# Attention and channel mix on one core: units of two pairs in one cycle, the receptance unit ahead of the last keys' scores, two gather steps on VectorE

## The chip, the cores and the metric

The kernel runs on one core of one Trainium2 chip. The metric is the device time of one execution in microseconds (us); three executions give a median. The profile is of one further execution. TensorE (PE in the profile) multiplies, with its weight loads shown apart as PEld; VectorE is DVE, ScalarE is ACT, SyncE (SP) issues all loads and stores, GpSimd (POOL) does almost nothing here.

## The reference

```python
# q, k, v: (8, 12, 448, 64); x: (8, 448, 768) after the heads are joined
scores = q @ k.transpose(0, 1, 3, 2) / sqrt(64) - log(448)
x = sigmoid(scores) @ v                       # heads joined to 768 columns
x_prev = x shifted by one row, first row zero
xk = mu_k * x + (1 - mu_k) * x_prev
xr = mu_r * x + (1 - mu_r) * x_prev
k  = maximum(xk @ w_k, 0)                     # 768 -> 1024
v  = k * k @ w_v                              # 1024 -> 768
r  = 1 / (1 + exp(-(xr @ w_r)))               # 768 -> 768, "receptance"
out = r * v
```

The scores carry a sigmoid and no sum over a row, so each block of keys can be weighed alone.

## The kernel before

Two heads make a pair: 48 pairs, six to each of the eight batch entries. Keys are cut into three chunks of 128 and a tail of 64. For one pair, `scores` (L322) multiplies a chunk of keys with all 448 queries of both heads, three times, because each operand is split into a high half and a low half (`kh`, `kl`, `qh`, `ql`; `prepare`, L295 the cast on ScalarE, L296 the rest on VectorE). The two heads use the two halves of the array's rows (64x128 in the profile). The result lies in a tile `sc` of two PSUM banks, one per head; there are three such tiles, used in turn. `sigmoid` (L343, ScalarE) turns it into `pf`. `score_tail` (L331) does the 64 last keys of both heads in one 128x128 multiplication into bank 0 of the next `sc`, and its sigmoid makes `pt`. `weigh` (L351) multiplies `pf` with the values into `av`, in 128x64 halves; `weigh_tails` (L360) adds the tails of two pairs in 64x64 quarters. So four shapes of the array are in use, and the order decides how often the shape changes.

`gather` takes a finished pair out of `av`: a copy `xx` (L369) and its store to `x_d`, a multiplication by 1 - mu_r into `t` (L371), the addition of the shifted part (L372, VectorE), and the split into `xr` high (L374, ScalarE) and low (L375, VectorE). The copy and the multiplication are on ScalarE.

`receptance` is one unit of xr @ w_r: six blocks of three matmuls (L386 to L388), 18 in all, into bank 1 of the `sc` tile whose bank 0 has the tail's scores; then a sigmoid `ro` (L392) and a store to `r_d`. 48 units are needed; 40 are done one per pair from pair 7 on, the other eight behind attention.

Meanwhile the weights, stored as 64-bit numbers, are turned into 32-bit ones by VectorE (`convert`, L222 to L226, from the raw words `wraw`), w_r first (L243, L244 split it into `slot`), then w_k and w_v, which `convert_seven` combines to the seven products of a fast matrix multiplication and stores to HBM. `load_weight` fetches such a product back (`wop`), and L411 and L412 split it into a slot.

Behind attention a second plan prepares the first right-hand sides (`ys`, `rr`) and runs the last eight units. A third plan is the channel mix itself (L592), both stages.

The order is not written by hand. Each step is entered in a plan with an engine, a cost in ns and a due time (`at`, counted in pairs); `Plan.order` runs a list schedule over the engines, lowest due time first, and emits the instructions in that order. TensorE's steps are chained, so their order is that in which the program enters them. Waits follow from the tiles, and a tile counts as a whole: a matmul that writes bank 1 of an `sc` tile waits for an earlier emitted sigmoid that reads bank 0 of it. Each engine takes its instructions strictly in order.

Of the kernel before, what the change touches and what calls it, by code (L numbers as in the profile page):

```python
# [8 lines left out]
F32 = mybir.dt.float32  # L9
# [88 lines left out]
def attention_then_channel_mix(  # L98
# [15 lines left out]
    P = 128  # L114
# [36 lines left out]

    WP, PFB, PTB, LEAD = 512, 6, 4, 2
    WR_PACE, W_PACE = 0.45, 0.75
    LATE = 2
# [157 lines left out]

    def turn(n, c):
        return (n * (NC + 1) + c) % 3

    def scores(n, c, at):
        u = turn(n, c)

        def go():
            for e, (kk, qq) in enumerate(products(n)):  # L320
                for h in range(2):
                    nc.tensor.matmul(sc[u][:, h, :S], kk[half[h], c * P:(c + 1) * P], qq[half[h], :], start=e == 0, stop=e == 2)  # L322

        pe(mm(3) + SWITCH * (c == 0), go, qk(n), [("sc", u, 0), ("sc", u, 1)], at)

    def score_tail(n, at):
        u = turn(n, NC)

        def go():
            for e, (kk, qq) in enumerate(products(n)):  # L330
                nc.tensor.matmul(sc[u][:, 0, :S], kk[:, NC * P:], qq, start=e == 0, stop=e == 2)  # L331

        pe(mm(3) + SWITCH, go, qk(n), [("sc", u, 0)], at)

    def sigmoid(n, c, at):
        u = turn(n, c)
        if c < NC:
# [8 lines left out]
    def weigh(n, c, at):  # L346
# [5 lines left out]

        pe(900 + SWITCH * (c == 0), go, [("pf", i), ("vn", n % 5)], [("av", n % 2)], at)


    def weigh_tails(n, at):
# [5 lines left out]
        reads = [x for m in (n, n + 1) for x in (("pt", m % PTB), ("vn", m % 5))]  # L362
        pe(950, go, reads, [("av", 0), ("av", 1)], at)

    def gather(n, at):
        b, j = divmod(n, NP)
        x, y = xx[n % 2], t1[n % 2]
        X, T = ("xx", n % 2), ("t1", n % 2)
        op(ACT, act(S), at, lambda: nc.scalar.copy(x[:, 1:], av[n % 2][:, :S]), [("av", n % 2)], [X])  # L369
        dma(x_d[j][b], x[:, 1:], at, [X], [("x_d", n)])  # L370
        op(ACT, act(S, True, True), at, lambda: nc.scalar.mul(y, x[:, :S], omr[:, j:j + 1]), [X, ("om", 0)], [T])  # L371
        op(DVE, dve(S, ptr=True), at, lambda: nc.vector.scalar_tensor_tensor(y, x[:, 1:], mur[:, j:j + 1], y, ALU.mult, ALU.add), [X, T], [T])  # L372
# [4 lines left out]
    def receptance(b, i, at, bank):  # L377
# [3 lines left out]
        for j in range(NJ):  # L381
# [8 lines left out]
            nh = i * P // HN  # L390
            pe(mm(3), go, keys + [("wr", j, nh), (("wr", j, nh), "lo")], [tk], at)
        op(ACT, act(S), at, lambda: nc.scalar.activation(ro[u], t[:, :S], AF.Sigmoid), [tk], [("ro", u)])  # L392
        dma(r_d[i][b], ro[u], at, [("ro", u)], [("r_d", i, b)])

# [21 lines left out]
    prepare(0, -9)  # L416
    load(1, -8)
    for i, (t, src, om) in enumerate(((mur, mu_r, omr), (muk, mu_k, omk))):
        dma(t, src, -2, [], [("mu", i)])
        op(DVE, 75, 0, lambda t=t, om=om: nc.vector.tensor_scalar(om, t, -1.0, 1.0, ALU.mult, ALU.add), [("mu", i)], [("om", i)])  # L420
    jt = 0.0
    for nh in range(2):
        for j in range(NJ):
            convert_wr(j, nh, jt)
            jt += WR_PACE
    jt = max(6, jt)
    for w, out7, half_rows, n in ((w_k, wk_o, NJH, DF // 2), (w_v, wv_o, NFH, HN)):
# [280 lines left out]
```

## Time and profile before

| | us |
|---|---|
| three executions | 930.02, 929.22, 929.09 |
| median | 929.22 |
| profiled execution, its own time | 932.01 |
| span of that execution | 930.2 |
| mean granted clock of TensorE | 0.99 |

The page's slices show the stages (each digit is the busy share of 1/40 of the span in tenths):

```profile
PE   6889999999999999999989999999999999999998
DVE  5999877852222232222225789696968978695955
ACT  5785666655565666556555756556464533233330
DMA  7679997863333434334127556334365556465514
```

Attention fills the first 21 slices, about 480 us. VectorE and the DMA engines are heavily used only in the first eight or nine of them, where the weights are converted. From slice 22 on the channel mix keeps TensorE full. A wait is given with the instruction that ended it; a group of instructions with its mean duration in ns and the idle time of the engine ahead of it. The time of a matmul is from its start to a modelled end, and matmuls overlap: the distance from one start to the next tells what one costs.

### The profile page before, as it was taken

What the parts mean: (1) busy time and instruction counts of PE and PEld (TensorE: products, weight loads), DVE (VectorE), ACT (ScalarE), POOL (GpSimd) and SP (SyncE); (2) the same over time, 40 slices, a digit from 0 to 9 for tenths busy, and PEclk for the clock granted to TensorE, in tenths of its full rate; (3) what the DMA queues carried; (4) which work ended last, traced back from release to release, by engine and by line L of the source; (5) the groups of instructions that cost most, each with busy time, mean ns of one, the idle gap of its engine ahead of it and who ended that gap; (6) DMA issues with size and microseconds to landing.
All of it is one profiled execution on the core that took longest, in us unless ns stands there. A gap on an engine that the chain in (4) does not pass through costs nothing.

```text
span 930.2 us, 13102 instructions
## 1 busy us (share of the span) xinstructions
PE 879.8 (95%) x4656; PEld 684.6 (74%) x4656; DVE 572.9 (62%) x1039; ACT 500.4 (54%) x858; POOL 0.5 (0%) x8
## 2 busy tenths in 40 slices
PE   6889999999999999999989999999999999999998
PEld 3446566656665666566558899999999999999997
DVE  5999877852222232222225789696968978695955
ACT  5785666655565666556555756556464533233330
POOL 0000000000000000000000000000000000000000
PEclk8899999999999999999999999999999999999999
DMA  7679997863333434334127556334365556465514
GB/s 257 205 252 335 302 318 241 280 215 102 122 115 103 135 111 132 102 106 130 50 92 245 175 174 197 119 139 129 125 228 161 199 163 216 132 196 178 159 60 148
DMA packets 90929, 159.21 MB, mean 171 GB/s; under 512 B 10352, under 2 KB 73328, under 8 KB 90864
## 3 DMA queue, kind: packets, MB, share of 16 engines
q1 hardware_dynamic: 90864, 158.38, 52.6%
q8 instruction: 36, 0.59, 0.3%
q14 instruction: 29, 0.24, 0.1%
HBM read 99.62 MB, written 58.72 MB: 170 GB/s over the span
## 4 chain that ended last, share of the span: by engine, by line
PE 91%; ACT 4%; DVE 2%; issue 2%; DMA 1%; SPq 0%; POOLq 0%; POOL 0%; ACTq 0%; DVEq 0%
PE xb L592 25%; PE yb L592 19%; PE av L351 12%; PE sc L322 10%; PE sc L386 7%; PE sc L388 6%; PE sc L387 6%; PE sc L331 4%; ACT pt L343 2%; PE av L360 2%; DMA wraw<-in_moe_w_r 1%; DVE wbits L226 0%; SPq L210 0%; ACT t L371 0%; ACT pf L343 0%
## 5 line engine op out<-in xcount | busy, mean ns | idle before, releaser
L386 PE MATMUL sc<-xr,slot 128*128 128x448 f32 x288 | 110.7, 384 | 30.9 <-ACT pt L343 25.3
L517 ACT CAST rr<-ys 128x448 fp32r<-128x448 f32 x135 | 73.9, 567 | 105.0 <-PE yb L592 40.6
L343 ACT ACTIVATE pf<-sc 128x896 f32<-128x896 f32 x144 | 122.7, 920 | 12.7 <-PE sc L322 12.7
L351 PE MATMUL av<-pf,vn 128*64 128x448 f32 x576 | 121.4, 557 | 0.0
L372 DVE SCALAR_TENSOR_TENSOR t<-xx,mur,t 128x448 f32<-128x448 f32 x48 | 30.7, 681 | 136.7 <-ACT t L371 136.7
L387 PE MATMUL sc<-xr,slot 128*128 128x448 f32 x288 | 105.9, 368 | 0.0
L388 PE MATMUL sc<-xr,slot 128*128 128x448 f32 x288 | 105.8, 367 | 0.0
L592 PE MATMUL xb<-rr,slotb 128*128 128x448 f32 x450 | 93.4, 365 | 0.7 <-issue 0.7
L592 PE MATMUL yb<-rr,slot 128*128 128x448 f32 x450 | 93.9, 364 | 0.0
L296 DVE TENSOR_TENSOR kl<-kn,kh 128x512 fp32r<-128x512 f32 x48 | 33.1, 690 | 97.2 <-ACT kh L295 97.2
L386 PEld LDWEIGHTS sc<-xr,slot 128*128 128x128 f32 x288 | 54.4, 189 | 51.8 <-ACT pt L343 40.2
L518 DVE TENSOR_TENSOR rr<-ys,rr 128x448 fp32r<-128x448 f32 x135 | 80.4, 618 | 19.5 <-ACT rr L517 19.4
L592 PEld LDWEIGHTS xb<-rr,slotb 128*128 128x128 f32 x450 | 84.4, 188 | 7.7 <-issue 1.1
L592 PEld LDWEIGHTS yb<-rr,slot 128*128 128x128 f32 x450 | 84.4, 187 | 6.7
L351 PEld LDWEIGHTS av<-pf,vn 128*64 128x64 f32 x576 | 37.8, 139 | 61.5 <-issue 60.4
L322 PE MATMUL sc<-qh,kh 64*128 64x448 f32 x288 | 59.6, 410 | 7.5 <-ACT qh L295 6.6
L392 ACT ACTIVATE ro<-sc 128x448 f32<-128x448 f32 x48 | 26.2, 545 | 67.4 <-PE sc L388 59.9
L322 PE MATMUL sc<-ql,kh 64*128 64x448 f32 x288 | 55.1, 379 | 6.0 <-DVE ql L296 6.0
L343 ACT ACTIVATE pt<-sc 128x448 f32<-128x448 f32 x48 | 26.1, 545 | 60.7 <-PE sc L388 55.7
L388 PEld LDWEIGHTS sc<-xr,slot 128*128 128x128 f32 x288 | 54.5, 189 | 4.6
L387 PEld LDWEIGHTS sc<-xr,slot 128*128 128x128 f32 x288 | 54.6, 190 | 3.6
L322 PE MATMUL sc<-qh,kl 64*128 64x448 f32 x288 | 54.1, 372 | 1.1 <-DVE kl L296 1.1
(88 smaller groups left out, 1410.0 us busy)
## 6 DMA issues: line engine op xcount, KB each, us to landing
k_d<-cc SPq DMA_DIRECT2D x64, 224.0 KB, 2.0
kn<-in_k SPq DMA_DIRECT2D x48, 256.0 KB, 2.7
qn<-in_q SPq DMA_DIRECT2D x48, 224.0 KB, 3.2
vn<-in_v SPq DMA_DIRECT2D x48, 224.0 KB, 3.1
x_d<-xx SPq DMA_DIRECT2D x48, 224.0 KB, 3.2
r_d<-ro SPq DMA_DIRECT2D x48, 224.0 KB, 2.6
x<-x_d SPq DMA_DIRECT2D x48, 224.0 KB, 2.6
rt<-r_d SPq DMA_DIRECT2D x48, 224.0 KB, 2.9
```

Of the source, the lines that this page charges most:

```text
L296: op(DVE, dve(w), at, lambda src=src, hi=hi, lo=lo: nc.vector.tensor_sub(lo[i], src[n % 2], hi[i]), [(a + "n", n % 2), (a + "h", i)], [(a ...
L322: nc.tensor.matmul(sc[u][:, h, :S], kk[half[h], c * P:(c + 1) * P], qq[half[h], :], start=e == 0, stop=e == 2)
L331: nc.tensor.matmul(sc[u][:, 0, :S], kk[:, NC * P:], qq, start=e == 0, stop=e == 2)
L343: op(ACT, act(w), at, lambda: nc.scalar.activation(f, s, AF.Sigmoid, bias=NEG_LOG_S, scale=SCALE), R, [K])
L351: nc.tensor.matmul(av[n % 2][half[h], :S], vn[n % 5][:, h * NC + c, :], pf[i][:, h, :], start=c == 0, stop=False)
L372: op(DVE, dve(S, ptr=True), at, lambda: nc.vector.scalar_tensor_tensor(y, x[:, 1:], mur[:, j:j + 1], y, ALU.mult, ALU.add), [X, T], [T])
L386: nc.tensor.matmul(t[:, :S], wr_hi[j][:, rows], hi, start=(j == 0), stop=False)
L387: nc.tensor.matmul(t[:, :S], wr_lo[j][:, rows], hi, start=False, stop=False)
L388: nc.tensor.matmul(t[:, :S], wr_hi[j][:, rows], lo, start=False, stop=(j == NJ - 1))
L517: op(ACT, act(S, True), at, lambda: nc.scalar.copy(r[:, 0], y), [Y], [R])
L518: op(DVE, dve(S), at, lambda: nc.vector.tensor_sub(r[:, 1], y, r[:, 0]), [Y, R], [R + ("lo",)])
L592: nc.tensor.matmul(bank[:, :S], a, b, start=first and t == 0 and e == 0, stop=t == n - 1 and e == 2, skip_group_check=True)
```

## The change

TensorE's steps of two pairs are entered as one cycle: scores of the odd pair, two receptance units, the tails of both pairs, scores of the next even pair, values of both pairs, tail values of both. A unit now stands ahead of the tail's scores that share its tile, and its `ro` sigmoid is entered behind those scores. Units start with pair 8, two per cycle. `sc` tiles are dealt out by a running count. There are nine `pf` buffers instead of six and three sets of high and low halves instead of two; loads and splits of the first pairs come earlier. From pair 10 on the copy and the multiplication of `gather` are on VectorE. The conversions have later due times, and the plan's costs of the value steps are 752 instead of 900 and 950. No weight product is fetched back during attention: all four slots are filled in the plan behind it, in memory that attention leaves.

```diff
-    WP, PFB, PTB, LEAD = 512, 6, 4, 2
-    WR_PACE, W_PACE = 0.45, 0.75
+    WP, PFB, PTB, LEAD = 512, 9, 4, 3
+    WR_PACE, W_PACE = 0.85, 0.9
+    R_FROM = 10
...
-    ka = ctx.enter_context(tc.tile_pool(name="ka", bufs=1, side="right"))
-    slots = ring(ka, "slotb", 2, [P, 2 * WO], F32R)
-    wop = ring(ka, "wop", 1, [P, WO], F32)
...
-        pe(mm(3) + SWITCH, go, qk(n), [("sc", u, 0)], at)
+        pe(mm(3), go, qk(n), [("sc", u, 0), ("tail", u)], at)
...
-        op(ACT, act(S), at, lambda: nc.scalar.copy(x[:, 1:], av[n % 2][:, :S]), [("av", n % 2)], [X])
+        if n < R_FROM:
+            op(ACT, act(S), at, lambda: nc.scalar.copy(x[:, 1:], av[n % 2][:, :S]), [("av", n % 2)], [X])
+        else:
+            op(DVE, dve(S), at, lambda: nc.vector.tensor_copy(x[:, 1:], av[n % 2][:, :S]), [("av", n % 2)], [X])
...
-        op(ACT, act(S, True, True), at, lambda: nc.scalar.mul(y, x[:, :S], omr[:, j:j + 1]), [X, ("om", 0)], [T])
+        if n < R_FROM:
+            op(ACT, act(S, True, True), at, lambda: nc.scalar.mul(y, x[:, :S], omr[:, j:j + 1]), [X, ("om", 0)], [T])
+        else:
+            op(DVE, dve(S, True, True), at, lambda: nc.vector.tensor_scalar(y, x[:, :S], omr[:, j:j + 1], None, ALU.mult), [X, ("om", 0)], [T])
...
-        op(ACT, act(S), at, lambda: nc.scalar.activation(ro[u], t[:, :S], AF.Sigmoid), [tk], [("ro", u)])
-        dma(r_d[i][b], ro[u], at, [("ro", u)], [("r_d", i, b)])
+        def out():
+            op(ACT, act(S), at, lambda: nc.scalar.activation(ro[u], t[:, :S], AF.Sigmoid), [tk, ("tail", tk[1])], [("ro", u)])
+            dma(r_d[i][b], ro[u], at, [("ro", u)], [("r_d", i, b)])
+
+        return out
...
+    load(2, -7)
...
-    jt = max(6, jt)
+    jt = max(R_FROM, jt)
...
-    for n in range(N + 1):
-        if n + 2 < N:
-            load(n + 2, n + 0.2)
-        if n < N:
-            if n + 1 < N:
-                prepare(n + 1, n + 0.6)
-            for c in range(NC):
-                scores(n, c, n)
-                sigmoid(n, c, n + 0.1 * c)
-        if n:
-            for c in range(NC):
-                weigh(n - 1, c, n)
-            if n % 2 == 0:
-                weigh_tails(n - 2, n)
-                gather(n - 2, n + 0.45)
-                gather(n - 1, n + 0.5)
-        if n < N:
-            score_tail(n, n)
-            sigmoid(n, NC, n + 0.5)
-        if n > NP and units:
-            b, i = units.pop(0)
-            u = turn(n, NC)
-            receptance(b, i, n + 0.4, (sc[u][:, 1], ("sc", u, 1)))
+    def key_chunks(n, at):
+        if n + 1 < N:
+            prepare(n + 1, at + 0.6 - 5 * (n < 4))
+        us = [turn() for _ in range(NC)]
+        for c in range(NC):
+            scores(n, c, us[c], at)
+            sigmoid(n, c, us[c], at + 0.1 * c)
+
+    key_chunks(0, 0)
+    for n in range(0, N, 2):
+        at = n + 1
+        key_chunks(n + 1, at)
+        if n + 3 < N:
+            load(n + 3, at + 0.2 - 5 * (n < 4))
+        us = [turn(), turn()]
+        done = []
+        for u in us:
+            if n >= 8 and units:
+                done.append(receptance(*units.pop(0), at + 0.4, (sc[u][:, 1], ("sc", u, 1))))
+        for i in range(2):
+            score_tail(n + i, us[i], at)
+        for f in done:
+            f()
+        for i in range(2):
+            sigmoid(n + i, NC, us[i], at + 0.5)
+        at = n + 2
+        if n + 2 < N:
+            key_chunks(n + 2, at)
+        for i in range(2):
+            for c in range(NC):
+                weigh(n + i, c, at)
+        weigh_tails(n, at)
+        if n + 4 < N:
+            load(n + 4, at + 0.2 - 5 * (n < 4))
+        gather(n, at + 0.45)
+        gather(n + 1, at + 0.5)
     late = units + late
-    for g in range(2):
-        load_weight(0, ORDER[g], N - 6 + 3 * g)
...
-    slots += ring(kp, "slotc", 2, [P, 2 * WO], F32R) + wr_slots
-    wop += ring(kp, "wopb", 1, [P, WO], F32)
+    slots = ring(kp, "slotb", 4, [P, 2 * WO], F32R) + wr_slots
+    wop = ring(kp, "wop", 2, [P, WO], F32)
...
-        if g >= 2:
-            load_weight(0, ORDER[g], 10 * g)
+        load_weight(0, ORDER[g], 10 * g)
```

Three places show what moves. In each row the number behind a name is that of the buffer, the one behind the underscore an identifier of the program; a wait names only the engine or DMA queue waited for.

TensorE before, in the steady part of attention, an odd pair: the tail's scores, then a receptance unit (`xr` by `slot`) in the same tile.

```order
L331 MATMUL sc0_286<-qh1_265,kh1_269 128x448 [waits Activation_49]
L331 MATMUL sc0_286<-qh1_265,kl1_271 128x448
L331 MATMUL sc0_286<-ql1_267,kh1_269 128x448
L386 MATMUL sc0_286<-xr0_236,slot0_233 128x448
L387 MATMUL sc0_286<-xr0_236,slot0_233 128x448
L388 MATMUL sc0_286<-xr0_236,slot0_233 128x448
L386 MATMUL sc0_286<-xr1_237,slot0_233 128x448 [waits Activation_49]
```

The fourth matmul of the unit waits for ScalarE. TensorE now, at the same place of a cycle: the end of the second unit, both tails, the next scores.

```order
L389 MATMUL sc2_289<-xr5_235,slot2_229 128x448
L390 MATMUL sc2_289<-xr5_235,slot2_229 128x448
L328 MATMUL sc1_288<-qh1_259,kh1_265 128x448
L328 MATMUL sc1_288<-qh1_259,kl1_268 128x448
L328 MATMUL sc1_288<-ql1_262,kh1_265 128x448
L328 MATMUL sc2_289<-qh2_260,kh2_266 128x448
L328 MATMUL sc2_289<-qh2_260,kl2_269 128x448
L328 MATMUL sc2_289<-ql2_263,kh2_266 128x448
L321 MATMUL sc0_287<-qh0_258,kh0_264 128x448 [waits Activation_49]
```

The tails stand behind both units, and no matmul of a unit but its first is marked with a wait.

ScalarE before, one cycle of two pairs, from the copy out of `av` to the next pair's first `pf`.

```order
L369 COPY xx0_282<-av0_289 128x448 [waits DMAHW7_49,PE_49,Activation_49]
L369 COPY xx1_283<-av1_290 128x448 [waits DMAHW0_49,PE_49,Activation_49]
L371 ACTIVATE t10_284<-xx0_282,omr_65 128x448 [waits DVE_49,Activation_49]
L371 ACTIVATE t11_285<-xx1_283,omr_65 128x448 [waits DVE_49,Activation_49]
L343 ACTIVATE pt2_280<-sc2_288 128x448 [waits PE_49]
L374 CAST xr0_236<-t10_284 128x448 [waits DVE_49]
L295 CAST kh0_268<-kn0_257 128x512 [waits DMAHW1_49]
L374 CAST xr1_237<-t11_285 128x448 [waits DVE_49]
L295 CAST qh0_264<-qn0_255 128x448 [waits DMAHW3_49]
L392 ACTIVATE ro1_243<-sc2_288 128x448 [waits DMAHW2_49,PE_49]
L343 ACTIVATE pf3_275<-sc0_286 128x896 [waits PE_49]
```

ScalarE now, part of one cycle: from the last two of the four casts for coming pairs to the first `pf` behind the tails.

```order
L293 CAST kh1_265<-kn0_251 128x512 [waits DMAHW0_49,Activation_49]
L293 CAST qh1_259<-qn0_249 128x448 [waits DMAHW1_49,Activation_49]
L339 ACTIVATE pf0_270<-sc2_289 128x896 [waits PE_49]
L339 ACTIVATE pf1_271<-sc0_287 128x896 [waits PE_49]
L339 ACTIVATE pf2_272<-sc1_288 128x896 [waits PE_49]
L376 CAST xr0_230<-t10_285 128x448 [waits DVE_49]
L376 CAST xr1_231<-t11_286 128x448 [waits DVE_49]
L396 ACTIVATE ro0_236<-sc2_289 128x448 [waits DMAHW6_49,PE_49,Activation_49]
L339 ACTIVATE pt2_281<-sc2_289 128x448
L396 ACTIVATE ro1_237<-sc0_287 128x448 [waits DMAHW7_49,PE_49,Activation_49]
L339 ACTIVATE pt3_282<-sc0_287 128x448
L339 ACTIVATE pf3_273<-sc1_288 128x896 [waits PE_49]
```

The copies and multiplications are gone from this queue, the `xr` casts wait for VectorE, and a unit's `ro` comes ahead of the `pt` of its tile, both behind the tails' scores.

ScalarE before, where attention has ended: `ys` starts a right-hand side, `slotc` is a weight slot, `ro0` and `ro1` belong to the first two of the eight last units.

```order
L374 CAST xr5_241<-t11_285 128x448 [waits DVE_49]
L504 ACTIVATE ys0_3671<-x20_3669,omk_66 128x448 [waits DMAHW6_49,DMAHW7_49,DMAHW5_49,Pool_49]
L392 ACTIVATE ro0_242<-sc0_286 128x448 [waits DMAHW1_49,PE_49]
L504 ACTIVATE ys1_3672<-x21_3670,omk_66 128x448 [waits DMAHW0_49,Pool_49]
L517 CAST rr0_3686<-ys0_3671 128x448 [waits DVE_49]
L411 CAST slotc0_3666<-wop0_223 128x768 [waits DMAHW1_49]
L517 CAST rr1_3687<-ys1_3672 128x448 [waits DVE_49]
L411 CAST slotc0_3666<-wop0_223 128x768 [waits DMAHW2_49]
L392 ACTIVATE ro1_243<-sc0_286 128x448 [waits DMAHW4_49,PE_49]
```

ScalarE now, at the same place.

```order
L376 CAST xr5_235<-t11_286 128x448 [waits DVE_49]
L417 CAST slotb0_3655<-wop0_3659 128x768 [waits DMAHW2_49,DMAHW3_49,DMAHW1_49,DMAHW5_49,DMAHW0_49,DMAHW6_49,DVE_49,PE_49]
L396 ACTIVATE ro0_236<-sc0_287 128x448 [waits DMAHW7_49,PE_49]
L417 CAST slotb0_3655<-wop0_3659 128x768 [waits DMAHW4_49]
L522 ACTIVATE ys0_3663<-x20_3661,omk_66 128x448 [waits DMAHW5_49,Pool_49]
L522 ACTIVATE ys1_3664<-x21_3662,omk_66 128x448 [waits DMAHW6_49,Pool_49]
L535 CAST rr0_3678<-ys0_3663 128x448 [waits DVE_49]
L417 CAST slotb1_3656<-wop1_3660 128x768 [waits DMAHW7_49]
L535 CAST rr1_3679<-ys1_3664 128x448 [waits DVE_49]
```

The first half of a weight slot, loaded through `wop0`, has moved ahead of the first `ro0`, and the `ys` steps follow it.

More of the change, by code (lines that the diff above doesn't have):

```diff
@@ L310, in qk, with turn, scores @@
         return [(a, i) for a in ("kh", "kl", "qh", "ql")]
[L313 to L317, printed above, removed]
+    turns = [0]
+    def turn():
+        turns[0] += 1
+        return (turns[0] - 1) % 3
+    def scores(n, c, u, at):
         def go():
@@ L324, in scores, with score_tail @@
         pe(mm(3) + SWITCH * (c == 0), go, qk(n), [("sc", u, 0), ("sc", u, 1)], at)
-    def score_tail(n, at):
-        u = turn(n, NC)
+    def score_tail(n, u, at):
         def go():
@@ L331, in go, with sigmoid @@
                 nc.tensor.matmul(sc[u][:, 0, :S], kk[:, NC * P:], qq, start=e == 0, stop=e == 2)
-        pe(mm(3) + SWITCH, go, qk(n), [("sc", u, 0)], at)
-    def sigmoid(n, c, at):
-        u = turn(n, c)
+        pe(mm(3), go, qk(n), [("sc", u, 0), ("tail", u)], at)
+    def sigmoid(n, c, u, at):
         if c < NC:
@@ L351, in go @@
                 nc.tensor.matmul(av[n % 2][half[h], :S], vn[n % 5][:, h * NC + c, :], pf[i][:, h, :], start=c == 0, stop=False)
-        pe(900 + SWITCH * (c == 0), go, [("pf", i), ("vn", n % 5)], [("av", n % 2)], at)
+        pe(752 + SWITCH * (c == 0) * (n % 2 == 0), go, [("pf", i), ("vn", n % 5)], [("av", n % 2)], at)
     def weigh_tails(n, at):
@@ L362, in weigh_tails @@
         reads = [x for m in (n, n + 1) for x in (("pt", m % PTB), ("vn", m % 5))]
-        pe(950, go, reads, [("av", 0), ("av", 1)], at)
+        pe(752, go, reads, [("av", 0), ("av", 1)], at)
     def gather(n, at):
@@ L390, in receptance @@
             nh = i * P // HN
-            pe(mm(3), go, keys + [("wr", j, nh), (("wr", j, nh), "lo")], [tk], at)
-        op(ACT, act(S), at, lambda: nc.scalar.activation(ro[u], t[:, :S], AF.Sigmoid), [tk], [("ro", u)])
-        dma(r_d[i][b], ro[u], at, [("ro", u)], [("r_d", i, b)])
+            pe(mm(3) + SWITCH * (j == 0), go, keys + [("wr", j, nh), (("wr", j, nh), "lo")], [tk], at)
+        def out():
+            op(ACT, act(S), at, lambda: nc.scalar.activation(ro[u], t[:, :S], AF.Sigmoid), [tk, ("tail", tk[1])], [("ro", u)])
+            dma(r_d[i][b], ro[u], at, [("ro", u)], [("r_d", i, b)])
+        return out
     ORDER = (0, 1, 5, 4, 6, 2, 3)
@@ L433, in attention_then_channel_mix @@
     units = units[:len(units) - LATE]
-    for n in range(N + 1):
+    def key_chunks(n, at):
[23 more added lines that the diff above has]
+        at = n + 2
         if n + 2 < N:
-            load(n + 2, n + 0.2)
-        if n < N:
-            if n + 1 < N:
-                prepare(n + 1, n + 0.6)
+            key_chunks(n + 2, at)
+        for i in range(2):
             for c in range(NC):
-                scores(n, c, n)
-                sigmoid(n, c, n + 0.1 * c)
-        if n:
-            for c in range(NC):
-                weigh(n - 1, c, n)
-            if n % 2 == 0:
-                weigh_tails(n - 2, n)
-                gather(n - 2, n + 0.45)
-                gather(n - 1, n + 0.5)
-        if n < N:
-            score_tail(n, n)
-            sigmoid(n, NC, n + 0.5)
-        if n > NP and units:
-            b, i = units.pop(0)
-            u = turn(n, NC)
-            receptance(b, i, n + 0.4, (sc[u][:, 1], ("sc", u, 1)))
+                weigh(n + i, c, at)
[4 more added lines that the diff above has]
+        gather(n + 1, at + 0.5)
     late = units + late
-    for g in range(2):
-        load_weight(0, ORDER[g], N - 6 + 3 * g)
     for t in xx:
@@ L556, in attention_then_channel_mix @@
     for u, (b, i) in enumerate(units):
-        receptance(b, i, 10 * u, banks[u % 6])
+        receptance(b, i, 10 * u, banks[u % 6])()
     with tc.manual_schedule():
```

## The prediction

> **What bounds the kernel now.** I read the page first: the span, the busy shares and the chain that ended last.
>
> ```profile
> span 930.2 us, 13102 instructions
> PE 879.8 (95%) x4656; PEld 684.6 (74%) x4656; DVE 572.9 (62%) x1039; ACT 500.4 (54%) x858; POOL 0.5 (0%) x8
> PE 91%; ACT 4%; DVE 2%; issue 2%; DMA 1%; SPq 0%; POOLq 0%; POOL 0%; ACTq 0%; DVEq 0%
> ```
>
> TensorE bounds it, so only time that TensorE loses can be won. The second view is busy time by stage: start-up until the last keys' scores of pair 8, one cycle of two pairs, the receptance units behind attention, the channel mix.
>
> ```profile
> 0.00:76.27 76.27, 61.03 (x333) 32.35 (x333) 63.32 (x136) 53.37 (x88) 0.33 (x6) 0.91 0.77 247
> 302.15:322.63 20.48, 19.21 (x111) 12.55 (x110) 4.81 (x8) 12.23 (x21) 0.00 (x0) 1.00 0.36 116
> 479.39:517.97 38.58, 32.27 (x148) 27.97 (x145) 20.30 (x31) 20.05 (x36) 0.13 (x2) 0.96 0.62 204
> 517.97:930.20 412.23, 408.08 (x2016) 378.16 (x2016) 326.69 (x573) 184.74 (x339) 0.00 (x0) 1.00 0.50 162
> ```
>
> The columns behind the length are PE, PEld, DVE, ACT and POOL busy with counts, granted clock, DMA share and GB/s. The last stage is solid matmul and the change leaves its order alone: 412.2 us stay. Third, the waits (total, times, longest) and one cycle of TensorE by the timeline (start, length):
>
> ```profile
> PE sc L386 <- ACT pt L343: 25.3, 40, 0.6
> ```
>
> ```profile
> 301.64 0.47 PE L331 MATMUL sc<-qh,kh 128*128 128x448 f32 x1
> ...
> 304.97 0.47 PE L386 MATMUL sc<-xr,slot 128*128 128x448 f32 x1 [0.63 <-ACT pt L343]
> 305.28 0.37 PE L387 MATMUL sc<-xr,slot 128*128 128x448 f32 x1
> ...
> 306.70 0.37 PE L388 MATMUL sc<-xr,slot 128*128 128x448 f32 x1
> 307.00 0.47 PE L322 MATMUL sc<-qh,kh 64*128 64x448 f32 x2
> ...
> 309.02 2.48 PE L351 MATMUL av<-pf,vn 128*64 128x448 f32 x12
> 311.43 0.47 PE L331 MATMUL sc<-qh,kh 128*128 128x448 f32 x1
> ...
> 316.78 0.47 PE L322 MATMUL sc<-qh,kh 64*128 64x448 f32 x2
> ...
> 318.80 2.48 PE L351 MATMUL av<-pf,vn 128*64 128x448 f32 x12
> 321.21 0.98 PE L360 MATMUL av<-pt,vn 64*64 64x448 f32 x8
> 322.12 0.47 PE L331 MATMUL sc<-qh,kh 128*128 128x448 f32 x1
> ```
>
> Three things are to be seen. A matmul starts every 0.203 us (305.28 to 306.70, seven steps). Where the tiling changes, the start-to-start is 0.30 (306.70 to 307.00) and the next 0.31: about 0.2 per change, 0.19 in the sums; a cycle has seven changes. And the receptance unit stops once per pair for the `pt` sigmoid: the stretch 301.64 to 307.00 is 5.36 for 21 matmuls, which need 21 x 0.203 + 0.19 = 4.45, so a stop costs **0.91**, not only the 0.63 of idle.
>
> **The steady cycle.** The changed order has, per two pairs, scores (18 slots in two groups), two units and two tails in one tiling (42 slots), 24 value matmuls, 8 tail-value matmuls: five tiling changes and no wait inside a unit. From the rows: scores 2 x 2.02 (307.00 to 309.02) = 4.04; units and tails 42 x 0.203 + 0.19 = 8.72; values 2 x 2.41 - 0.19 = 4.63; tail values 0.91 (321.21 to 322.12). Sum **18.30** against 20.48 (two stops of 0.91 and two changes of 0.19 gone).
>
> What is late next is ScalarE behind the units:
>
> ```profile
> 304.38 0.54 ACT L343 ACTIVATE pt<-sc 128x448 f32<-128x448 f32 x1 [0.50 <-PE sc L388]
> 304.82 0.56 ACT L374 CAST xr<-t 128x448 fp32r<-128x448 f32 x1
> 307.91 2.54 ACT L343 ACTIVATE pf<-sc 128x896 f32<-128x896 f32 x3 [0.26 <-PE sc L322]
> ```
>
> Back to back, such an instruction follows after 0.44; three `pf` take 2.54, and the first starts 0.91 after the first score. Counted from a cycle's first score (0), the units start at 2.02 (the first `pf` ends at 1.8, so no wait), the tails at 9.43, and their last matmuls end at 10.20 and 10.81. ScalarE then runs ro, pt, ro, pt from 10.25: they end at 10.80, 11.24, 11.68, 12.12. The next scores start at 10.75 with a free bank; the second chunk wants its bank at 11.46 (free at 11.29), the third at 12.07 (free at 12.17). One small stop, 0.15 with the restart: cycle **18.45**. The casts for the next two pairs end at 16.5 and their low halves on VectorE at 17.2, wanted at 18.3.
>
> **VectorE's two steps.** The trace of before has neither. Nearest rows:
>
> ```profile
> L624 DVE TENSOR_TENSOR u<-yb,p1s 128x448 f32<-128x448 f32 x28 | 17.4, 621 | 14.7 <-PE yb L592 14.4
> L223 DVE TENSOR_SCALAR wexpo<-wraw 128x384 uint32<-128x384 uint32 (+1 forms) x40 | 15.1, 378 | 0.0
> ```
>
> A copy out of PSUM lies between 0.38 and 0.62; I take 0.55, near the row that reads PSUM. The multiply lies in the same bounds; I take 0.45. That adds 2.0 to VectorE's 4.81 per cycle, hidden under 18.4. What waits for them are the two `xr` casts, ahead of the first `ro` in ScalarE's queue: ready at 3.3 of the cycle, queued for 10.2, so 6 us of cover; if it is gone, each us more is a us of TensorE. The units read a batch gathered a cycle or more earlier.
>
> **Start-up.** Rows of ScalarE, VectorE and TensorE:
>
> ```profile
> 6.57 0.62 ACT L295 CAST kh<-kn 128x512 fp32r<-128x512 f32 x1 [2.01 <-DMA kn<-in_k]
> 9.89 0.36 DVE L222 TENSOR_SCALAR wbits<-wraw 128x384 uint32<-128x384 uint32 x1 [1.64 <-DMA wraw<-in_moe_w_r]
> 38.33 0.74 PE L322 MATMUL sc<-ql,kh 64*128 64x448 f32 x2 [1.00 <-DVE ql L296]
> 41.24 3.90 PE L351 MATMUL av<-pf,vn 128*64 128x448 f32 x12
> 76.27 0.47 PE L331 MATMUL sc<-qh,kh 128*128 128x448 f32 x1
> ```
>
> Between 6.57 and 9.89 three loads landed (224, 224, 384 KB): 0.25 MB/us. The moved loads put 2080 KB ahead of pair 2's keys, which land at 12, and the first raw weights at 14.5 instead of 9.9. From there I walked the first cycles by the durations above. The scores no longer wait for low halves (paces 0.85 and 0.9, a third buffer). Instead ScalarE is late: six `pf`, two `pt`, four casts, the gather's six steps and two weight casts are 11.6 us per cycle against 11.0 of matmul, and the copies and multiplies stand ahead of a `pf` that the tails wait for. Cycles of about 13.8: tail values of pairs 2 and 3 end at 37, of 6 and 7 at 64, the first unit starts at **67**. Before stands at the same work at 73.7 (76.27, less the unit it has done, 18 x 0.203 + 0.91 = 4.55, plus the scores of pair 9, 2.02). Ends: 60 without a wait, 73.7 with none saved. One cycle more pays 1.0, because pairs 8 and 9 are still gathered on ScalarE.
>
> A clock-gate rule bears here. In the trace, the wait of 1.00 at 38.33 was followed by matmuls at half rate: 2.91 until the value matmuls, where seven slots and a change need 1.6, and 3.90 for those instead of 2.48, so 2.7 lost. The Trainium skill, "TensorE: Matmul & The Clock Gate", section "Why this matters for your kernels", allows gaps of up to about 3 us; by it, no start-up wait of mine (2.5 at most) slows the clock, and 883 stands; by the trace, shorter waits close together can, and it would be 886. The measurement goes first; 886 is inside the range.
>
> **The stretch behind attention.** Rows of TensorE, ScalarE and the DMA queue:
>
> ```profile
> 478.47 0.98 PE L360 MATMUL av<-pt,vn 64*64 64x448 f32 x8
> 483.78 0.80 SPq L210 DMA_DIRECT2D x<-x_d  x2
> 486.37 0.67 ACT L504 ACTIVATE ys<-x,omk 128x448 f32<-128x448 f32 x1 [3.38 <-DMA x<-x_d]
> 487.52 0.47 PE L386 MATMUL sc<-xr,slot 128*128 128x448 f32 x1 [3.54 <-ACT ro L392]
> 489.86 0.83 ACT L411 CAST slotc<-wop 128x768 fp32r<-128x768 f32 x1 [1.37 <-DMA wop<-wk_o]
> 491.49 0.83 ACT L411 CAST slotc<-wop 128x768 fp32r<-128x768 f32 x1 [0.33 <-DMA wop<-wk_o]
> ```
>
> Attention's last matmul ends at 479.45; `ro` of the first unit waits in ScalarE's queue behind a step that waits for a 224 KB load, and TensorE resumes 8.07 later. The change puts a 384 KB load and its cast there: 0.65 for 160 KB more, 0.2 for the longer cast, 0.2 for a gather that ends later, so about 9.1; three more matmuls run ahead of the wait (0.6). Net +0.4. The two weights formerly loaded during attention add 1.57 MB: at 384 KB in 1.63 us (489.86 to 491.49) up to 6.6 if the loads bound it, nothing if 29 us of units hide them. I take +0.6: 38.5 becomes **39.5**, ends 38.5 to 45.
>
> **Sum.** 67 + 1.0 + 19 x 18.45 (350.6) + the last cycle's units, tails and values 14.3 (8.72 + 4.63 + 0.98) + 39.5 + 412.2 = 884.6 of span. The profiled execution took 932.01 with a span of 930.2; the median, 929.22, is 2.8 below it. So 884.6 + 1.8 - 2.8 = 883.6, called **883**.
>
> **The rivals.**
> - *Start-up smooth, no stop in the cycle, loads hidden:* 61 + 19 x 18.30 + 14.3 + 38.5 + 412.2, less 1.0 for the median: 873. For it, VectorE has room; against it, 0.77 of DMA share in that stage.
> - *ScalarE's evacuation becomes the bound.* If the four instructions behind the tails follow at their own length, 0.55, instead of 0.44, the last is 0.33 later and both chunks wait: some 0.6 more per cycle, 19 x 0.6 = 11, 894. Their ACT total (12.23 of 20.48) speaks against more. The Trainium skill, "TensorEngine Tiling (Array Packing)", section "PSUM Bottleneck", warns of this: a faster TensorE does not speed up what empties PSUM. No row of before shows four such instructions in a row.
> - *VectorE late in the cycles that convert weights:* the low halves have 1.1 us of slack; about nine such cycles, each 1.3 us behind that slack, are 12: 895.
> - *The gather holds ScalarE, and the kernel is slower.* If VectorE, behind conversions that wait for raw weights, delivers the gather over 6 us late, the `xr` casts hold ro and pt, and the scores wait for their banks. The change has 46 us to lose, 2.3 in each of 20 cycles: from 8.3 us late in every cycle it is slower, at 10 us 963. Against it: most cycles have no conversion left.
> - *The stop inside the unit stays* (the wait sits elsewhere in the tile's dependences): 40 x 0.91 = 36 back, 919, and with bad luck in the stretch no change. Against it: the rows of the changed order mark no wait there.
>
> **How the numbers follow.** Forecast 883 (876 to 890) 0.65; smooth 873, 0.12; evacuation 0.09; late low halves 0.08; gather 0.03; stop stays 0.03. The range, 870 to 897, holds the first four and the open ends of start-up (7 down, 7 up) and of the loads (1 down, 5.5 up). A measurement tells about 0.2% from no change here. Faster by more than that 0.96, within 0.01, slower 0.03.
>
> **What would show it.** Right: no row of receptance waiting for `pt`; a steady cycle of 18.3 to 18.6 from one L356 group to the next; the first unit at 60 to 74; 38 to 45 from attention's end to the first channel-mix matmul. Wrong: a cycle above 19 (then see what `sc` waits for), TensorE waiting for `ql` in the converting cycles, or half-rate matmuls beyond the start.

## The result, and the profile after

The changed kernel takes **885.88 us** (median of four executions, 884.61 to 886.42) against 929.62 for the kernel before, run beside it (929.09 to 931.51): a ratio of 0.9524, with a 95% interval of 0.9506 to 0.9542. The forecast was 883.0, the range 870 to 897. The profiled execution took 885.37 with a span of 883.6.

The page of the changed kernel, its span and busy times:

```profile
span 883.6 us, 13116 instructions
PE 858.4 (97%) x4656; PEld 686.0 (78%) x4656; DVE 606.1 (69%) x1115; ACT 450.1 (51%) x782; POOL 0.5 (0%) x8
```

The same four stages as before (start-up to the first unit, one cycle of two pairs, attention's end to the first channel-mix matmul, the channel mix), with the same columns:

```profile
0.00:65.04 65.04, 51.90 (x333) 28.30 (x333) 53.53 (x116) 55.27 (x95) 0.33 (x6) 1.00 0.78 247
305.51:324.08 18.57, 18.57 (x115) 12.75 (x112) 6.59 (x12) 9.68 (x16) 0.00 (x0) 1.00 0.39 134
433.28:472.16 38.88, 31.95 (x146) 27.82 (x145) 25.51 (x39) 20.54 (x36) 0.13 (x2) 0.96 0.72 240
472.16:883.60 411.44, 407.28 (x2016) 378.00 (x2016) 326.70 (x573) 184.76 (x339) 0.00 (x0) 1.00 0.50 162
```

TensorE is now busy for all of the 18.57 of a cycle (19.21 of 20.48 before). One such cycle by the timeline, TensorE first, where L321 is the scores, L388 the unit, L328 the tails, L347 the values and L356 the tail values:

```profile
305.51 0.47 PE L321 MATMUL sc<-qh,kh 64*128 64x448 f32 x2
...
307.53 0.47 PE L388 MATMUL sc<-xr,slot 128*128 128x448 f32 x1
...
314.94 0.36 PE L328 MATMUL sc<-qh,kh 128*128 128x448 f32 x1
...
316.24 0.47 PE L321 MATMUL sc<-qh,kh 64*128 64x448 f32 x2
...
317.36 0.37 PE L321 MATMUL sc<-ql,kh 64*128 64x448 f32 x2
317.70 0.47 PE L321 MATMUL sc<-qh,kh 64*128 64x448 f32 x2
...
318.50 4.73 PE L347 MATMUL av<-pf,vn 128*64 128x448 f32 x24
323.16 0.98 PE L356 MATMUL av<-pt,vn 64*64 64x448 f32 x8
324.08 0.47 PE L321 MATMUL sc<-qh,kh 64*128 64x448 f32 x2
```

Between 307.53 and 316.24 stand 42 matmuls without a stop. Of the waits of a whole execution (total, times, longest) these two are a unit's, and neither is for `pt`:

```profile
PE sc L388 <- ACT ro L396: 6.2, 4, 4.2
PE sc L388 <- ACT pf L339: 2.0, 2, 1.0
```

The four for `ro` lie behind attention, the two for `pf` in the first two cycles with units. The one irregular step of the cycle is from 317.36 to 317.70: 0.34 instead of 0.203, and the matmul behind it 0.31. That is the third chunk, which waits for its bank. ScalarE in the same cycle shows for what:

```profile
315.80 0.54 ACT L396 ACTIVATE ro<-sc 128x448 f32<-128x448 f32 x1 [5.91 <-issue]
316.24 0.54 ACT L339 ACTIVATE pt<-sc 128x448 f32<-128x448 f32 x1
316.66 0.55 ACT L396 ACTIVATE ro<-sc 128x448 f32<-128x448 f32 x1
317.09 0.56 ACT L339 ACTIVATE pt<-sc 128x448 f32<-128x448 f32 x1
```

The four instructions follow at 0.44, 0.42 and 0.43, and the last ends at 317.65, 0.05 before the third chunk starts.

The longer waits of the start-up, and those of the first two cycles with units:

```profile
24.80 0.47 PE L328 MATMUL sc<-qh,kh 128*128 128x448 f32 x1 [1.38 <-ACT pf L339]
...
38.11 0.47 PE L328 MATMUL sc<-qh,kh 128*128 128x448 f32 x1 [1.01 <-ACT pf L339]
...
40.26 0.47 PE L328 MATMUL sc<-qh,kh 128*128 128x448 f32 x1 [1.29 <-ACT pf L339]
...
65.04 0.47 PE L388 MATMUL sc<-xr,slot 128*128 128x448 f32 x1 [0.98 <-ACT pf L339]
...
84.78 0.47 PE L388 MATMUL sc<-xr,slot 128*128 128x448 f32 x1 [1.01 <-ACT pf L339]
```

The wait for low halves on VectorE, which cost a half-rate stretch before, is gone; TensorE waits for `pf` instead. Behind attention:

```profile
437.98 0.36 PE L390 MATMUL sc<-xr,slot 128*128 128x448 f32 x1
442.50 0.74 PE L388 MATMUL sc<-xr,slot 128*128 128x448 f32 x1 [4.15 <-ACT ro L396]
...
468.07 0.47 PE L388 MATMUL sc<-xr,slot 128*128 128x448 f32 x1 [0.68 <-ACT ro L396]
...
472.16 14.64 PE L609 MATMUL xb<-rr,slotb 128*128 128x448 f32 x72 [0.73 <-issue]
```

```profile
441.17 0.83 ACT L417 CAST slotb<-wop 128x768 fp32r<-128x768 f32 x1 [4.18 <-DMA wop<-wk_o]
441.90 0.54 ACT L396 ACTIVATE ro<-sc 128x448 f32<-128x448 f32 x1
```

`ro` stands behind a cast that waits for a weight load, and the next unit, in the other bank of the same tile, waits for `ro`. TensorE resumes 9.22 after attention's end.

### The profile page after: what moved, and what is told of

The parts are those of the page before. It is cut to its first block, busy times and chain, and to the rows that moved or that the text cites. A ratio compares the mean times of both kernels' runs of the same rounds, so it can differ in the third digit from the quotient of the medians.

```text
span 883.6 us, 13116 instructions
## 1 busy us (share of the span) xinstructions
PE 858.4 (97%) x4656; PEld 686.0 (78%) x4656; DVE 606.1 (69%) x1115; ACT 450.1 (51%) x782; POOL 0.5 (0%) x8
## 4 chain that ended last, share of the span: by engine, by line
PE 92%; ACT 4%; issue 1%; DMA 1%; DVE 1%; SPq 0%; ACTq 0%; POOLq 0%
PE xb L609 26%; PE yb L609 20%; PE av L347 12%; PE sc L321 10%; PE sc L388 7%; PE sc L389 6%; PE sc L390 6%; PE sc L328 3%; PE av L356 2%; ACT pf L339 2%; ACT t L371 1%; DMA kn<-in_k 1%; ACT xr L376 0%; DMA wop<-wk_o 0%; ACT qh L293 0%
## 5 line engine op out<-in xcount | busy, mean ns | idle before, releaser
L609 PE MATMUL xb<-rr,slotb 128*128 128x448 f32 x675 | 138.7, 362 | 0.7 <-issue 0.7
L609 PEld LDWEIGHTS xb<-rr,slotb 128*128 128x128 f32 x675 | 126.5, 187 | 9.7 <-issue 1.1
L388 PE MATMUL sc<-xr,slot 128*128 128x448 f32 x288 | 108.7, 377 | 8.2 <-ACT ro L396 6.2
L347 PE MATMUL av<-pf,vn 128*64 128x448 f32 x576 | 113.5, 543 | 0.0
L347 PEld LDWEIGHTS av<-pf,vn 128*64 128x64 f32 x576 | 39.2, 137 | 63.0 <-issue 61.1
L388 PEld LDWEIGHTS sc<-xr,slot 128*128 128x128 f32 x288 | 54.4, 189 | 20.7 <-ACT pf L339 8.3
L321 PE MATMUL sc<-qh,kh 64*128 64x448 f32 x288 | 60.5, 417 | 6.7 <-ACT qh L293 5.0
L321 PEld LDWEIGHTS sc<-qh,kh 64*128 64x128 f32 x288 | 27.3, 186 | 39.8 <-issue 21.2
L321 PE MATMUL sc<-ql,kh 64*128 64x448 f32 x288 | 53.4, 367 | 0.0
L321 PE MATMUL sc<-qh,kl 64*128 64x448 f32 x288 | 53.1, 365 | 0.0
L527 DVE TENSOR_TENSOR ys<-ys,ys 128x448 f32<-128x448 f32 x76 | 45.0, 618 | 0.1
```

Of the source, the lines that this page charges most:

```text
L347: nc.tensor.matmul(av[n % 2][half[h], :S], vn[n % 5][:, h * NC + c, :], pf[i][:, h, :], start=c == 0, stop=False)
L388: nc.tensor.matmul(t[:, :S], wr_hi[j][:, rows], hi, start=(j == 0), stop=False)
L527: op(DVE, dve(S), at, lambda: nc.vector.tensor_sub(d, x, y), [X, Y], [D_])
L609: nc.tensor.matmul(bank[:, :S], a, b, start=first and t == 0 and e == 0, stop=t == n - 1 and e == 2, skip_group_check=True)
```

## The experiments

Each kernel ran beside the kernel before on one chip. That kernel's median was 931.6 to 932.7 there; the changed kernel's ratio is 0.9524. Single executions of the kernel before lie between 928.60 and 933.13, which blurs every ratio, while the traces repeat well: a steady cycle of 18.57 and matmuls of the channel mix that take 407.28 from the first start to the last end stand in the changed kernel and in several of its variants. So where two ratios lie close, the traces are read. Tail-value rows (L356; L360 in kernels made from the one before) mark a cycle.

### The stop alone: taken away from the kernel before, put back into the changed one

```diff
 # before: unit first, tail behind it, ro behind the tail
+            done = receptance(...)
         if n < N:
             score_tail(n, n)
+            if done:
+                done()
             sigmoid(n, NC, n + 0.5)
-            receptance(...)
```

> The kernel before, with one edit: each receptance unit is entered ahead of the tail's scores that share its tile, and its ro behind them. Order of pairs, tilings, buffers, gather on ScalarE and weight loads stay as before. Theory (the stop inside the unit is worth 0.91 each, and most of the gain): 40 x 0.91 = 36 less than before, about 893 us, no row of L386 to L388 waiting for pt, two pairs in 18.7 us instead of 20.48. Rival (the gain is in the fewer tiling changes, in VectorE's two steps or in the start-up): 920 to 929 us. Second rival (ScalarE is then the limit, because it still has the copies and multiplications of the gather): the stop goes, but scores or units wait for pf instead, 900 to 915 us.

Measured: 899.42 us, ratio 0.9669 [0.9646, 0.9693]. No row of the unit waits for `pt`. A cycle, by its first unit and the next cycle's:

```profile
299.95 0.47 PE L386 MATMUL sc<-xr,slot 128*128 128x448 f32 x1
...
318.80 0.47 PE L386 MATMUL sc<-xr,slot 128*128 128x448 f32 x1
```

18.85 instead of 20.48: 1.63 of the 1.82 that two stops of 0.91 make, 32 us of the whole. So a move of a few lines gives some 70% of the gain of the change. ScalarE, with all of the gather, did not become the limit here.

```diff
 # changed kernel: tail ahead of its unit again, pair by pair
-        for u in us:
+        for i, u in enumerate(us):
+            score_tail(n + i, u, at)
+            sigmoid(n + i, NC, u, at + 0.5)
             if n >= 8 and units:
-                done.append(receptance(...))
-        ...                       # tails, ro and pt of both pairs
+                receptance(*units.pop(0), at + 0.4, (sc[u][:, 1], ("sc", u, 1)))()
```

> The changed kernel, with the tail's scores of each pair entered ahead of the unit that shares their tile, tail and unit alternating; the cycle of two pairs with its five tiling changes, the gather on VectorE and all buffers stay. Theory: two stops of 0.91 come back in each of 20 cycles, 36 us, about 922 us; two pairs take 20.2 to 20.4 us. Rival (the stop is worth only its idle time of 0.63, the rest of the gain is in tilings): 25 us, about 911. Rival (the place of the unit does nothing): 886.

Measured: 920.74, ratio 0.9899 [0.9876, 0.9923]. The waits of the page, and two cycle marks:

```profile
PE sc L388 <- ACT pt L339: 24.1, 38, 0.6
```

```profile
307.42 0.98 PE L356 MATMUL av<-pt,vn 64*64 64x448 f32 x8
...
327.66 0.98 PE L356 MATMUL av<-pt,vn 64*64 64x448 f32 x8
```

A cycle is 20.24, 1.67 more than 18.57. The third chunk no longer stops here (the units' stops have let ScalarE catch up), so two stops cost 1.67 + 0.24 = 1.91, 0.96 each. The first theory holds and the 0.63 of idle alone would not give it. Both directions agree: the place of the unit is worth 32 to 35 us.

### VectorE's two steps

```diff
-    R_FROM = 10
+    R_FROM = 48      # all of the gather on ScalarE; in the second run 0, all on VectorE
-    jt = max(R_FROM, jt)
+    jt = max(10, jt)
```

> The changed kernel with the copy and the multiplication of all gathers on ScalarE; due times as they are. Theory: the four steps stand ahead of a pf that a unit or the tails wait for, as in the cycle with pairs 8 and 9, which took 1.2 us longer; 19 cycles, some 20 us more, about 906 us, with rows of L388 or L328 waiting for pf. Rival (in the steady cycle ScalarE has 5.9 us of idle time, so that VectorE's part is worth nothing): 886 us with a cycle of 18.6.

Measured: 905.94, ratio 0.9739 [0.9717, 0.9761]; `PE sc L388 <- ACT pf` is 20.2 us, once per cycle. ScalarE in a cycle of this run, and the unit that waits:

```profile
201.48 0.97 ACT L366 COPY xx<-av 128x448 f32<-128x448 f32 x2 [2.22 <-issue]
202.33 1.24 ACT L371 ACTIVATE t<-xx,omr 128x448 f32<-128x448 f32 x2
203.46 0.92 ACT L339 ACTIVATE pf<-sc 128x896 f32<-128x896 f32 x1
```

```profile
204.43 0.47 PE L388 MATMUL sc<-xr,slot 128*128 128x448 f32 x1 [1.01 <-ACT pf L339]
```

Copies and multiplications of two pairs hold the first `pf` back, and the unit needs its tile. That ScalarE later idles for 5.9 of the same cycle does not help: what counts is what stands ahead of `pf`.

> The kernel before with the unit ahead of the tail's scores (as in the run that took 899.4) and, in addition, the copy and the multiplication of the gather on VectorE from pair 10 on; one pair per cycle. Theory (VectorE's part is worth 20 us only where two pairs' evacuations come in a row; with one pair per cycle no unit and no score waits for pf in the steady state): no gain in the steady cycle, 18.7 to 18.85, 897 to 900 us. Rival (relief of ScalarE is worth the same anywhere): 880 to 885 us.

Measured: 896.99, ratio 0.9636 [0.9621, 0.9651]; a cycle of 18.67. The theory held; most of the 0.18 less than 18.85 is the spacing of the matmuls in the units, 0.203 here and 0.207 there. Four ratios stand side by side, all with the unit ahead of the tails:

| | gather on ScalarE | on VectorE from pair 10 |
|---|---|---|
| one pair per cycle, start-up of before | 0.9669 | 0.9636 |
| two pairs per cycle, start-up of the change | 0.9739 | 0.9524 |

VectorE's part is worth about 20 us in the lower row and some 3 in the upper one. Without it the two-pair cycle is a loss against the simple move of the unit.

> The changed kernel with the copy and the multiplication of all gathers on VectorE, from the first pair on; due times as they are. Theory: the waits of the tails for pf in the start-up (some 1 to 1.8 us per cycle of two pairs, four cycles) and the 1.2 of the cycle with pairs 8 and 9 go: 5 to 8 us less, 878 to 881 us, first unit at 58 to 60. Rival (VectorE, behind conversions that wait for raw weights, delivers the copy late, and the values wait for av): 886 to 895 us, with rows of L351 waiting for xx or for VectorE.

Measured: 885.29, ratio 0.9513 [0.9499, 0.9528]: no difference from 0.9524 that can be told. Both halves of the theory happened, and cancelled. The `pf` waits of the start-up went and the cycle behind pairs 8 and 9 took 18.51 instead of 19.73, but the first unit started at 65.65, not at 58 to 60, because in one earlier cycle VectorE was late, with low halves and not with `av`:

```profile
41.43 0.74 PE L321 MATMUL sc<-ql,kh 64*128 64x448 f32 x2 [4.37 <-DVE ql L294]
...
44.34 6.17 PE L347 MATMUL av<-pf,vn 128*64 128x448 f32 x24
```

The wait is followed by matmuls at half rate (24 values in 6.17 instead of 4.73).

### Tilings and start-up

```diff
 # values of the even pair ahead of the units: six tiling changes
         us = [turn(), turn()]
+        for c in range(NC):
+            weigh(n, c, at)
...
-        for i in range(2):
-            for c in range(NC):
-                weigh(n + i, c, at)
+        for c in range(NC):
+            weigh(n + 1, c, at)
```

> The changed kernel with the values of the even pair entered ahead of the units instead of behind the next scores: six tiling changes in a cycle instead of five. Theory (a change costs 0.19): 24 x 0.19 = 4.6 us more, about 890.5 us, the cycle 18.75. Rivals: nothing, if changes are free and the 0.2 seen at them is something else (886); more than 8 us, if the values then wait for pf.

Measured: 888.75, ratio 0.9526 [0.9511, 0.9541]. The ratio tells no difference from the change, but the traces do: attention's last group starts at 435.51 instead of 432.30, 3.2 later, and what follows takes the same time. A steady cycle is 18.86, 0.29 more, 5.5 us over 19 cycles: 0.14 for the extra change (24 value matmuls in two groups take 4.80 between starts instead of 4.66), the rest from units and tails, which take 8.87 there instead of 8.71, because their matmuls follow at 0.207. The first unit started at 60.88 instead of 65.04, which was not foreseen, and a later wait of 3.08 for `ql` made one cycle 4.8 longer, which took that back. So the price of a change lies between 0.14 and 0.29 here, which holds the 0.19 taken; that the time is near the theory's 890.5 owes something to two effects that it does not have.

```diff
-    WR_PACE, W_PACE = 0.85, 0.9
+    WR_PACE, W_PACE = 0.45, 0.75
```

> The changed kernel with the due times of the weight conversions as they were before (0.45 and 0.75 of a pair instead of 0.85 and 0.9). Theory (with faster conversions VectorE is behind in the start-up and the scores wait for low halves again): first unit 3 to 7 us later than 65.0, 889 to 893 us. Rival (the third set of halves alone keeps them ahead): 884 to 887 us.

Measured: 894.08, ratio 0.9585 [0.9570, 0.9601]; first unit at 72.08, 7.0 later, with 2.7 us of waits for `ql`. The theory holds, though the time is 1 us over its range: of the 8.7 won in the start-up, most hangs on the later due times.

> The changed kernel with two sets of high and low halves instead of three. Theory: the split of a pair can start only when the scores and tails of the pair two before are done, one cycle later than with three, and scores wait for ql or kl: 1 to 3 us in a cycle, 900 to 940 us. Rival (the third set is only a convenience): 886 us.

Measured: 890.67, ratio 0.9555 [0.9510, 0.9600]; no wait for `ql` or `kl`, first unit at 74.15, steady cycles 18.57 to 18.73. The waits of the theory did not come, but the run does not test it: with two sets (`LEAD` 2 instead of 3) the halves of pair n + 2 are entered ahead of the tail's scores of pair n, so the even pairs' tail scores are computed from another pair's halves, the output is wrong, and those scores hold no split back. The late first unit is no price of the third set either: the profiled execution, 895.94, is the slowest of four (the fastest took 887.60), with matmuls at half rate in three cycles of its start-up. In this order the third set is needed for the result; what it is worth in time the run does not say.

### Behind attention

```diff
-    banks = [... for i in range(3) for h in range(2)]
+    banks = [... for h in range(2) for i in range(3)]
```

> The changed kernel; behind attention the units are dealt to the six banks so that three units in a row are in three tiles, instead of two in a row in one tile. Nothing else moves on TensorE. Theory (the 4.15 wait for ro, the half rate after it and the three stops of 0.68 come from two units that share a tile): attention's end to the first channel-mix matmul 38.9 becomes 30 to 31 (8 x 18 x 0.203 = 29.2 and a stop), 877 to 878 us. Rival (the loads of the four weights and their casts bound the stretch, so that the wait goes elsewhere): the first channel-mix matmul waits for a slot or rr, stretch 35 to 39, 882 to 886 us.

Measured: 884.76, ratio 0.9489 [0.9472, 0.9506]. All waits of units for `ro` are gone, the units run through to 462.87, and then:

```profile
468.21 16.46 PE L609 MATMUL xb<-rr,slotb 128*128 128x448 f32 x72 [5.33 <-issue]
```

```profile
467.01 0.67 ACT L522 ACTIVATE ys<-x,omk 128x448 f32<-128x448 f32 x1 [0.72 <-DMA x<-x_d]
467.58 0.52 ACT L396 ACTIVATE ro<-sc 128x448 f32<-128x448 f32 x1
```

The channel mix takes over the banks of the last units, whose `ro` now stands behind multiplications that wait for `x_d`. The stretch is 34.9 instead of 38.9, and the half rate after the longer wait takes some back (72 matmuls in 16.46 instead of 14.64). By the time the rival won, and in that the wait came back further on; but what it came back at is the last `ro`, not a slot or a right-hand side.

```diff
-    AHEAD = 3
+    AHEAD = 2        # with the banks above
```

> The changed kernel with the units behind attention dealt to banks so that no two in a row share a tile, and in addition the third right-hand side (six loads of x_d and their work) moved from the plan behind attention to that of the channel mix. Theory (with the banks alone the stop moved to the first channel-mix matmul, which waited 5.33 for the last ro, because ScalarE was held by multiplications that wait for x_d): the last ro no longer stands behind them, stretch 38.9 becomes 30.5 to 32, 877 to 879 us. Rival (the loads are only late by a fixed amount, and the third product of the channel mix waits for its right-hand side instead): 882 to 885 us with a wait of L609 inside the channel mix.

Measured: 889.72, ratio 0.9562 [0.9546, 0.9578], slower than the changed kernel. The rival's mechanism won, at more than its price. TensorE entered the channel mix at 466.00, 6.2 earlier than the change, but the matmuls of the channel mix then took 417.7 instead of 407.3: the third product waited for its right-hand side, 7.4 us in four waits, and the next product's 36 matmuls took 8.27 instead of 7.36. The longest wait is

```profile
489.81 0.74 PE L609 MATMUL xb<-rrb,slotb 128*128 128x448 f32 x1 [4.75 <-ACT rrb L535]
```

> The run with banks and the moved right-hand side, and in addition two things of the start-up: the values of the even pair entered ahead of the tails for pairs 0 to 7 only (where the run with six tiling changes started its first unit 4.2 us earlier), and the gather on VectorE from pair 8 instead of 10. Theory: the first unit at 60 to 62 instead of 65.0 and the 1.2 of the cycle behind pairs 8 and 9 gone, 4 to 6 us less than the run with banks and the moved right-hand side. Rival (the earlier start meets VectorE's conversions, and later scores wait for ql by 3 to 4.5 us, as they did in two of the runs): 0 to 2 us less.

Measured: 884.13, ratio 0.9501 [0.9481, 0.9520], 5.6 us less than the run before. The first unit started at 59.13 and attention's last group at 425.39, where the changed kernel has 432.30: the start-up edits are worth 6.9 and the theory held. The moved right-hand side costs 7.6 us of waits for `rrb` here too.

```diff
+    for u, (b, i) in enumerate(units):       # was behind the loop of weights and right-hand sides
+        receptance(b, i, 10 * u, banks[u % 6])()
+    hold.append(("ro", (b * NJ + i) % 2))    # the last ro
...
 # fetch: multiplication by omk
-... [X], [Y])
+... [X] + (hold if role > 1 and t else []), [Y])
```

> The changed kernel with the units behind attention dealt to banks so that no two in a row share a tile, the two start-up edits of the run before (values of the even pair ahead of the tails for pairs 0 to 7, gather on VectorE from pair 8), the third right-hand side back in the plan behind attention, but with its multiplications from the third load on entered behind the last ro. Theory: attention ends 6.9 earlier as in the run before, TensorE enters the channel mix some 31 after attention's end (the last ro waits for two x_d loads at most, not four) and its third product finds its right-hand side: 885.9 - 6.9 - 4 to 7 = 872 to 875 us. Rival (the wait for the x_d loads cannot be moved, only its place: the third product or the copies out of xb wait instead): 877 to 880 us.

Measured: **873.47 us**, ratio 0.9378 [0.9362, 0.9394], against 931.81 for the kernel before. Attention's last group starts at 425.11, and then:

```profile
458.80 7.45 PE L614 MATMUL xb<-rr,slotb 128*128 128x448 f32 x36 [3.33 <-issue]
467.17 7.48 PE L614 MATMUL xb<-rr,slotb 128*128 128x448 f32 x36 [0.92 <-ACT p1s L643]
```

The stretch is 32.7 where the theory had some 31, the third product finds its right-hand side, and 0.92 is lost to a copy out of `xb`. The time is the forecast one; this version beats both kernels. The wait of 3.33 was not followed by half rate (36 matmuls in 7.45), as shorter ones were in other runs; the forecast did not count on that.

## Why the prediction was right, step by step

- **The stop inside the unit.** 0.91 each, gone in all 40 places. The runs give 0.82 (taken from the kernel before, in a run whose matmuls follow each other more slowly) and 0.96 (put back); the run with one pair per cycle and VectorE's part, at 0.203, gives (20.48 - 18.67) / 2 = 0.91. This is the cause of most of the gain: shown in both directions.
- **Two tiling changes fewer, 0.38 per cycle.** Right by two runs side by side: 18.67 with seven changes (one pair per cycle and VectorE's part), and 18.57 less the third chunk's stop of 0.24, so 18.33, with five: 0.17 a change for 0.19. In the change most of it is given back by the third chunk, so that the two-pair order itself wins 0.10 per cycle, 2 us in all.
- **The third chunk's stop** was mis-sized, 0.24 instead of 0.15: its group of scores takes 2.26 (316.24 to 318.50) instead of 2.02. ScalarE's chain came as forecast: the first `ro` started at 10.29 of the cycle for 10.25, and the last `pt` ended at 12.14 for 12.12. The chunk started 0.14 late, and the matmul behind it came after 0.31 instead of 0.203, so the restart costs 0.10, twice what was taken; the value matmuls took 4.66 for 4.63. Cycle 18.57 for 18.45, over 19 cycles 2.3 us. VectorE's copy and multiplication took 0.54 and 0.36 from start to start, for 0.55 and 0.45, and TensorE waited for neither in a steady cycle. The Trainium skill, "TensorEngine Tiling (Array Packing)", section "PSUM Bottleneck", advises to empty PSUM with ScalarE and VectorE together once TensorE is faster. The run with all of the gather on ScalarE agrees, with 20 us, of which the copy out of `av` is one part of two; with one pair per cycle VectorE's help is worth only some 3.
- **Start-up:** 65.0 for 67, by the mechanism named (tails that wait for `pf` behind the gather on ScalarE). The granted clock was 1.00 there, so the 886 of the slower clock did not come; the last section shows that waits like these were followed by half rate in another run. The cycle of pairs 8 and 9 cost 1.17 for 1.0.
- **Stretch behind attention:** 38.9 for 39.5. The resume came after 9.22 (about 9.1 forecast). Matmuls at half rate follow it, as they follow the wait in the kernel before (granted clock 0.96 in both stretches), so that the sum has them in its 38.5 without naming them; the 0.6 for loads was not needed.
- **Channel mix:** 411.4 for 412.2.
- **The sum** of the span was 884.6 and is 883.6. That it is so near is luck in part: the start-up came out 2.0 less, the cycles 2.3 more, the last two stages 1.4 less. The forecast of 883 lies 2.9 below the median because it took 2.8 off for the profiled execution of before, which had been that much above its median; the changed kernel's profiled execution is 0.5 below its own. That last term was the largest error. Executions of the kernel before took 928.60 at a granted clock of 0.997 and 933.06 at 0.988, and the start-up of the profiled one has 0.91, where the changed kernel has 1.00; so the 2.8 was probably half rate that the changed start-up does not have. This is argued, not tested.
- **Where the gain lies.** Of the 46.6 us between the two spans, 37.5 were won in attention's cycles with units, 8.7 in the start-up and 0.8 in the channel mix; 0.3 were lost behind attention.

Not settled: why matmuls of some runs follow at 0.207 and not 0.203 (18.85 against 18.67 with one pair per cycle; units and tails of 8.87 against 8.71 with six tiling changes). It was not tried. Nor did a run take away the nine `pf` buffers or the earlier loads alone.

## What to carry to other kernels

Where two writers share a tile, put the long one that is read late ahead of the short one that is read at once; a stop inside a stream costs more than the idle time that the profile shows (0.63 idle, 0.82 to 0.96 in all). Parts of a change are not additive: the two-pair order needed VectorE's help to be a gain at all. A wait that is removed should be followed to the next consumer of the same buffer: behind attention it came back twice before the queue that caused it was reordered.

## What the runs showed of the hardware

At half rate a matmul starts every 0.37 instead of every 0.203. It did not need one long wait. In the run with the earlier due times it came behind waits of 1.39 and 0.81 within 1.7 us, and lasted to 62.25:

```profile
57.49 0.47 PE L328 MATMUL sc<-qh,kh 128*128 128x448 f32 x1 [1.39 <-ACT pf L339]
...
59.17 0.74 PE L328 MATMUL sc<-qh,kh 128*128 128x448 f32 x1 [0.81 <-ACT pf L339]
59.71 0.58 PE L328 MATMUL sc<-qh,kl 128*128 128x448 f32 x1
```

Nor can it be told from the waits alone. The changed kernel's waits of 1.01 and 1.29, 2.2 us apart, did not bring it. Its waits of 1.38, 0.40 and 0.40, of which the last is the first row here, did not either:

```profile
27.35 0.47 PE L321 MATMUL sc<-qh,kh 64*128 64x448 f32 x2 [0.40 <-ACT pf L339]
27.66 0.36 PE L321 MATMUL sc<-qh,kl 64*128 64x448 f32 x2
```

The run with the moved right-hand side has the same start-up, with waits of 1.41, 0.40 and 0.33, and they did:

```profile
26.76 0.74 PE L321 MATMUL sc<-qh,kh 64*128 64x448 f32 x2 [0.33 <-ACT pf L339]
27.30 0.57 PE L321 MATMUL sc<-qh,kl 64*128 64x448 f32 x2
```

Where the channel mix begins, half rate followed a wait of 2.32 in the run with the two start-up edits (72 matmuls in 16.24 instead of 14.64), and none followed the wait of 3.33 in the last run. The Trainium skill, "TensorE: Matmul & The Clock Gate", section "Why this matters for your kernels", names a single gap of about 3 us; the waits of 4.15 and 4.37 above agree, these shorter ones and the 3.33 do not. What decides between like waits the runs do not show. A forecast with waits of 1 to 3 us on TensorE should therefore carry both outcomes in its range.
